# Local q and k in runs of six tokens, put in order on GpSimd, with a one-step scale for the values

## The chip, the cores and the metric

The kernel runs on one core of a Trainium2 chip. The metric is device time in microseconds, the median of three runs of the whole program: 700.77 us before the change (699.4 to 700.79). Five engines work beside each other, each with its own queue in program order: TensorE (PE; its weight loads are listed apart as PEld), VectorE (DVE), ScalarE (ACT), GpSimd (POOL), and SyncE (SP), which issues all DMAs of this kernel.

## What is computed

Attention over 4 batches, 8 heads, 576 tokens and 64 dimensions, with two kinds of mask, feeds two dense blocks. The first four heads are local (a token sees the 32 tokens up to itself); the other four are strided (a token sees the earlier tokens of its residue modulo 32).

```python
scores = scale * np.matmul(q, k.transpose(0, 1, 3, 2))
mask_local = (rel >= 0) & (rel < 32)
mask_strided = (rel >= 0) & (pos[None, :] % 32 == pos[:, None] % 32)
attn = softmax(where(mask, scores, -1e9)); x = attn @ v          # 2304 x 512
h = x @ w_in; sm = softmax(h); solu = h * sm                     # 2304 x 1024
ln = (solu - mu) / np.sqrt(var + 1e-06) * g_ln; y = ln @ w_out   # 2304 x 512
out = (y @ w_a * (y @ w_b)) @ w_out2                             # 512 -> 1536 -> 512
```

## The kernel before

**Tiling.** Attention works on pairs of heads. A `Group` is one batch and one pair, two of each four groups being local and two strided. For each group `load_qk` and `load_v` bring q, k and v into SBUF; `group_T` turns q and k on the PE (`rawq`, `rawk` to `qkT`, six transposes each, then a copy by ACT out of PSUM, L618 for local and L615 for strided groups); `att_tile` makes the scores (L696, L701), the softmax (DVE L719, L728, L732, L736, L738; ACT L731), the product with 1/sum on POOL (`e<-e,r`, L768 in batch 0, L777 later), the transposed probabilities `PT`, and the product with v on the PE into `xbank`. ACT copies this into `xT` (L825). In batch 0 the probabilities are transposed on the PE (L764) and copied by ACT (L774). In batches 1 to 3 they and v are each split into two f16 parts, `PT` comes by a transposing DMA, and v must first be scaled by a power of two.

**The scale of v.** `pair_scale`, once for every two groups of batches 1 to 3 (six times), reduces |v| over each partition into `am` (L630) and calls `pow2_scale`: a transpose on the PE (L500), a maximum on DVE (L501), a second transpose (L505), a second maximum (L506), three DVE instructions on one number (L511 to L513), a matmul that spreads the result over the partitions (L515), and a DVE product (L516). The PE writes these into `scp`, the upper part of the bank `xbank`, beside the attention products in its lower part `x`. The scale of the output weights (`scale_wout`) goes through the same steps once.

**After attention.** `moe1` takes 128 tokens from `xT`: ACT writes `xh` (L845) and DVE `xl` (L849), and 24 matmuls make `h` (L856). DVE, ACT and POOL form softmax, solu and normalisation (DVE L861, L871, L876); a transposing DMA brings `lnT`, and 96 matmuls for every 256 tokens make `y` (L910). The last stage multiplies by a Strassen-like scheme (L1326, L1472). Weights arrive as raw words: each piece of 512 KB goes through a ring of three buffers (`raw64`), is issued at L454, and converted by ACT (L455) and DVE (L461, L465); the pieces of `w_in` are then split by ACT (L474) and POOL (L475).

**Order.** `P.schedule` emits all operations in the order of the table `ISSUE`, which was written ahead of time. Each engine runs its share of that order without overtaking, so an instruction that waits holds all that stands behind it on its engine.

**Local loads before.** `load_qk` brings a local group by one DMA for each head and tensor: 96 partitions, six tokens in each, the tokens of one partition 96 apart, so a run in memory is one token of 256 B. Local transposes then read `rawq` and `rawk` at once.

Of the kernel before, what the change touches and what calls it, by code (L numbers as in the profile page):

```python
# [8 lines left out]
F32 = mybir.dt.float32  # L9
# [21 lines left out]
QT = 96  # L31
# [21 lines left out]
PARAM = dict(back=12, first=40, early=(0,), seed=4, noise=0.1, direct=((0, 0), (0, 1)), stay=0.0, pf1=(),  # L53
             pf2=(), ph1=(), pv=(), pp=(8,), ps1=(), ps2=(), ps3=False, ps4=False, passes=200, ysub=False, wsum=False, osum=False, plo2=(), so=(0, 1, 2), bM=8, bN=4, e=3,
             PT=3, raw=2, rawl=2, raws=2, qkT=2, V=2, wk=2, xt=1, ln=2, lnT=2, ys=2, raw64=3, f64f=4, att=100.0,
# [1572 lines left out]
```

## Time and profile before

| what | us |
|---|---|
| median of three runs | 700.77 |
| the profiled execution | 695.03 |
| its span, first to last instruction | 693.3 |
| PE busy in the span | 664.4 (96%) |
| DVE, ACT, POOL busy | 571.5, 447.2, 144.7 |

The profiled execution is 5.74 us shorter than the median of the timed runs. The page gives busy time for each engine; the windows give the same for a stretch, with the clock that the PE was granted (1.00 stands for 2.4 GHz, 0.50 for 1.2 GHz) and the DMA engines' busy share and rate; the timeline gives single instructions and, in brackets, the idle time ahead of one with what ended it.

### The profile page before, as it was taken

How to read it: one execution, taken by the hardware profiler on the slowest of the kernel's cores; microseconds unless marked ns; L12 is line 12 of the kernel's file. 1: busy time of each engine (PE TensorE's matmuls, PEld its weight loads, DVE VectorE, ACT ScalarE, POOL GpSimd, SP SyncE). 2: the span in 40 equal slices, each digit the busy share in tenths (PEclk: the TensorE clock that was granted, in tenths of full speed). 3: DMA queues.
4: the chain of work that ended last, by engine and by line, in shares of the span. 5: the costliest groups of instructions: out<-in, count | busy, mean ns of one | idle time of the engine just before them, and what ended most of it. 6: DMA issues, size and time to landing. Idle time of an engine off the chain costs nothing.

```text
span 693.3 us, 15572 instructions
## 1 busy us (share of the span) xinstructions
PE 664.4 (96%) x5991; PEld 498.8 (72%) x5991; DVE 571.5 (82%) x1238; ACT 447.2 (65%) x898; POOL 144.7 (21%) x268
## 2 busy tenths in 40 slices
PE   5987899999999999999999999999999999999997
PEld 4766677878787888886576676766767676775676
DVE  5789899789678644999999999799977989786576
ACT  3679868777767644986978787676543746434421
POOL 5544546536537432410000000000000000000000
PEclk9999899999999999999999999999999999999999
DMA  9999979999998434677254043653522304641023
GB/s 209 258 243 244 188 138 194 264 186 268 222 248 199 102 81 102 188 249 240 103 184 152 0 141 104 198 201 97 175 100 94 120 32 166 237 138 46 1 92 122
DMA packets 152650, 109.68 MB, mean 158 GB/s; under 512 B 101376, under 2 KB 131072, under 8 KB 152576
## 3 DMA queue, kind: packets, MB, share of 16 engines
q1 hardware_dynamic: 152576, 108.69, 60.4%
q8 instruction: 47, 0.77, 0.5%
q14 instruction: 27, 0.22, 0.1%
HBM read 65.41 MB, written 27.53 MB: 134 GB/s over the span
## 4 chain that ended last, share of the span: by engine, by line
PE 61%; DVE 8%; ACT 5%; issue 1%; POOL 0%; ACTq 0%; POOLq 0%
PE N L1326 17%; PE M L1326 13%; PE N L1472 9%; PE y L910 7%; PE M L1472 7%; PE h L856 6%; ACT y L1267 1%; DVE p L1423 1%; ACT w L1128 1%; DVE w L1132 1%; DVE y L1269 1%; DVE A L1415 1%; DVE A L1393 1%; DVE V L647 0%; ACT Z L1238 0%
## 5 line engine op out<-in xcount | busy, mean ns | idle before, releaser
L1326 PEld LDWEIGHTS <-w 128*128 128x128 f16 x1512 | 147.9, 98 | 91.7 <-issue 2.0
L1326 PE MATMUL N<-y,w 128*128 128x384 f16 x864 | 156.2, 326 | 0.7 <-ACT N L1333 0.7
L1472 PEld LDWEIGHTS <-p 128*128 128x128 f16 x1071 | 104.7, 98 | 20.4 <-issue 1.1
L1326 PE MATMUL M<-y,w 128*128 128x384 f16 x648 | 118.5, 326 | 0.8 <-ACT N L1333 0.8
L910 PE MATMUL y<-lnT,wout 128*128 128x256 f16 x864 | 101.4, 273 | 1.5 <-DMA lnT<-ln 0.8
L910 PEld LDWEIGHTS <-wout 128*128 128x128 f16 x864 | 82.0, 98 | 15.2 <-issue 4.1
L1418 ACT CAST p<-A 128x384 f16<-128x384 f32 x119 | 59.2, 512 | 40.1 <-DVE A L1393 22.6
L856 PE MATMUL h<-win,xh 128*128 128x512 f32 x288 | 79.8, 417 | 2.7 <-DVE wk L871 2.6
L1472 PE MATMUL N<-wo,p 128*128 128x256 f16 x612 | 77.7, 273 | 1.0 <-DVE yst L1488 1.0
L856 PEld LDWEIGHTS h<-win,xh 128*128 128x128 f32 x288 | 54.4, 198 | 14.4 <-DVE wk L871 3.3
L1423 DVE TENSOR_TENSOR p<-A,p 128x384 f16<-128x384 f32 x119 | 62.3, 552 | 2.7 <-ACT p L1418 2.7
L1472 PE MATMUL M<-wo,p 128*128 128x256 f16 x459 | 60.2, 273 | 0.0
L455 ACT ACTIVATE f64f<-raw 128x512 f32<-128x512 f32 x52 | 34.6, 674 | 11.2 <-DMA raw<-in_moe_w_in_dram 7.3
L856 PE MATMUL h<-win,xl 128*128 128x512 f32 x144 | 39.2, 394 | 0.0
L1415 DVE TENSOR_TENSOR A<-A 128x384 f32<-128x384 f32 x72 | 39.0, 553 | 0.2
L1488 DVE SCALAR_TENSOR_TENSOR ob<-M,osc,ob 128x256 f32<-128x256 f32 x63 | 27.8, 477 | 12.6 <-PE M L1472 11.1
L777 POOL TENSOR_TENSOR e<-e,r 128x324 f32<-128x324 f32 (+2 forms) x30 | 26.2, 881 | 50.0 <-DVE r L738 28.2
L861 DVE TENSOR_REDUCE st<-h 128x1 f32<-128x1024 f32 x18 | 22.0, 1220 | 17.2 <-PE h L856 17.1
L856 PEld LDWEIGHTS h<-win,xl 128*128 128x128 f32 x144 | 26.7, 188 | 5.9
L465 DVE SCALAR_TENSOR_TENSOR f64f<-f64f,raw 128x512 int32<-128x512 int32 x36 | 28.8, 804 | 2.3 <-ACT f64f L455 1.8
L1348 ACT COPY V<-M 128x384 f32<-128x384 f32 x36 | 17.0, 473 | 20.0 <-PE M L1326 19.9
L871 DVE SCALAR_TENSOR_TENSOR wk<-h,st,wk 128x1024 f32<-128x1024 f32 x18 | 23.0, 1279 | 7.8 <-POOL st L869 7.7
(191 smaller groups left out, 1207.0 us busy)
## 6 DMA issues: line engine op xcount, KB each, us to landing
raw<-in_moe_w_out_dram SPq DMA_DIRECT2D x20, 512.0 KB
o_scr<-ob SPq DMA_DIRECT2D x36, 256.0 KB
ob<-o_scr SPq DMA_DIRECT2D x30, 256.0 KB
raw<-in_moe_w_a_dram SPq DMA_DIRECT2D x12, 512.0 KB
raw<-in_moe_w_b_dram SPq DMA_DIRECT2D x12, 512.0 KB
y_scr<-y SPq DMA_DIRECT2D x14, 384.0 KB
y<-y_scr SPq DMA_DIRECT2D x14, 384.0 KB
y_scr<-ys SPq DMA_DIRECT2D x18, 256.0 KB
```

The lines of the kernel that those rows point to most:

```text
L455: act(0.67, lambda: nc.scalar.activation(f(), raw()[:, :, 1].bitcast(F32), AF.Prelu, scale=2.0 ** -112, alpha=-2.0 ** 32), (raw,), (f,))
L465: dve(0.77, lambda: nc.vector.scalar_tensor_tensor(g().bitcast(I32), f().bitcast(I32), 3, raw()[:, :, 0], op0=ALU.logical_shift_left, op1= ...
L777: pool(0.1 + 1.2 * pl, lambda: nc.gpsimd.tensor_tensor(ev(), ev(), r()[:, :ng].unsqueeze(2).to_broadcast([128, ng, nk]), op=ALU.mult), (r, ...
L856: nc.tensor.matmul(h()[:, 512 * n:512 * n + 512], xs[xa]()[:, kk], win[wa][:, kk, 512 * n:512 * n + 512], start=(pi == 0 and kk == 0), sto ...
L871: dve(1.3, lambda: nc.vector.scalar_tensor_tensor(e(), h(), st()[:, 7:8], e(), op0=ALU.mult, op1=ALU.mult, accum_out=st()[:, 2:3]), (h, (s ...
L910: nc.tensor.matmul(y()[:, 256 * mi:256 * mi + 256], wout[:, kk, wa, 128 * m:128 * m + 128], lnT()[:, xa, kk], start=(pi == 0 and kk == 0), ...
L1326: nc.tensor.matmul(to()[:, :HB], w()[:, wa, a, kk], y7[b]()[:, xa, kk], start=first and pi == 0 and kk == 0, stop=pi == 2 and kk == 1, ski ...
L1415: dve(TD, lambda: nc.vector.tensor_tensor(to(), x(), y(), op=op), toks, (to,))
L1418: act(0.5, lambda: nc.scalar.copy(pu(0, a), x()), (x,), (pu.tok(0, a),))
L1423: dve(TD, lambda: nc.vector.tensor_tensor(pu(1, a), x(), pu(0, a), op=ALU.subtract), (x, pu.tok(0, a)), (pu.tok(1, a),))
L1472: nc.tensor.matmul(bk(i), pus[u](xa, a)[:, 128 * tt:128 * tt + 128], wo()[:, u, b, wa], start=a == A11 and u == 0 and pi == 0, stop=u == U ...
L1488: dve(0.475, lambda: nc.vector.scalar_tensor_tensor(dst(), bk(i), s(), dst(), op0=ALU.mult, op1=ALU.add), (src, osc), (obt(t, c),))
```

## The change

A local group's q (and k) comes by one DMA: a partition gets six tokens that follow each other, so a run in memory is 1536 B. GpSimd copies the 96 x 768 block into a new buffer `rawx` with the heads side by side, the transposes read `rawx`, and the ACT copy out of PSUM puts the tokens in order. `rawx` has one buffer, used in turn by q and k of every local group: 16 copies in all. `pair_scale` no longer calls `pow2_scale`: two matmuls against a block of ones sum the partitions' maxima, so that each partition has the sum at once, and four DVE instructions make the power of two and its inverse. The PE output of both now stands in the ring `x`, one buffer that it shares with the attention products. `scale_wout` keeps its steps but also uses `x`. Estimates of PE times in the planner's calls are a little higher, and the table `ISSUE` is new from end to end: of its numbers nothing can be read; what it moves is shown below.

```diff
+    ring("at", "rawx", [QT, 2 * NM * D], F32, pm["rawx"])
...
-    ring("psR", "x", None, F32, 1).fixed = lambda n: xbank[:, :352]
-    ring("psR", "scp", None, F32, 1).fixed = lambda n: xbank[:, 352:]
+    ring("psR", "x", None, F32, 1).fixed = lambda n: xbank
...
-            for h in range(2):
-                dma(lambda t=t, h=h, src=src: nc.sync.dma_start(
-                    out=tokens(t)[:, :, h], in_=src[h].rearrange("(m p) d -> p m d", p=QT)), (), ((t, h),), 190000)
+            src = src.rearrange("h (p m) d -> p h (m d)", p=QT)
+            dma(lambda t=t, src=src: nc.sync.dma_start(out=t().rearrange("p (h n) -> p h n", h=2), in_=src),
+                (), ((t, 0), (t, 1)), 225000)
...
+            if not g.strided:
+                flat, raw = raw, rings["rawx"].new()
+                pool(0.95, lambda flat=flat, raw=raw: nc.gpsimd.tensor_scalar(
+                    raw().rearrange("p (m h d) -> p m h d", m=NM, h=2), flat().rearrange("p (h m d) -> p m h d", h=2, m=NM),
+                    1.0, 1.0, op0=ALU.mult, op1=ALU.mult), ((flat, 0), (flat, 1)), ((raw, 0), (raw, 1)))
...
-                    nc.scalar.activation(dst.rearrange("p (i t) -> p i t", i=2), src, AF.Copy, scale=sc)
+                    nc.scalar.activation(dst.rearrange("p (w i o) -> p w i o", i=2, o=NM // 2),
+                                         src.rearrange("p i (o w) -> p w i o", w=QT), AF.Copy, scale=sc)
...
-        pow2_scale(am, (am,), len(gs), 0, sc, sc)
+        tp, m1 = rings["x"].new(), rings["m1"].new()
+
+        def total():
+            for i in range(len(gs)):
+                nc.tensor.matmul(tp()[:, :1], ones_sq, am()[:, i:i + 1], start=i == 0, stop=i == len(gs) - 1)
+        pe(0.3, total, (am, "small"), (tp,))
+        dve(0.15, lambda: nc.vector.tensor_scalar(m1().bitcast(I32), tp()[:, :1].bitcast(I32), 0x7F800000, None,
+                                                  op0=ALU.bitwise_and), (tp,), (m1,))
+
+        def powers():
+            up, down = sc()[:, 0:1], sc()[:, 1:2]
+            nc.vector.tensor_scalar(down, m1(), 2.0 ** -14, 2.0 ** -60, op0=ALU.mult, op1=ALU.max)
+            nc.vector.reciprocal(up, down)
+            nc.vector.tensor_scalar(down, down, 1.0 / PSCALE, None, op0=ALU.mult)
+        dve(0.4, powers, (m1,), (sc,))
...
 ISSUE = [int(n) for n in """
-10 0 13 11 14 5 2 15 16 1 12 6 18 17 21 8 35 19 9 20 7 4 22 414 37 430 3 771 787 36 39 38 40 43 41 42 181 187 23 66 44
```

The line numbers behind the changed functions shift: by up to 16 from `att_tile` on (L774 is L790 in the changed kernel, L825 is L841, L845 is L861, L856 is L872, L803 is L819), and by one ahead of it (L455 is L454, L474 is L473).

The first place is ACT's queue ahead of the first `xh`, the input of the first `h`. In these rows `raw_407` and the like are raw weight pieces in the order of loading, `e` probabilities, `PT` transposed probabilities. The kernel before:

```order
L474 CAST win_108<-f64f 128x512
L774 COPY PT<-y 96x512
L455 ACTIVATE f64f<-raw_543 128x512
L731 ACTIVATE e_116<-e_116 128x192
L825 ACTIVATE xT<-xbank 128x256
L845 CAST xh<-xT 128x512
L474 CAST win_108<-f64f 128x512
L455 ACTIVATE f64f<-raw_619 128x512
```

Here `raw_543` is the eighth and last piece of `w_in` and `raw_619` the first of the output weights; the second one's conversion comes five rows further on. The changed kernel:

```order
L473 CAST win_108<-f64f 128x512
L454 ACTIVATE f64f<-raw_578 128x512
L790 COPY PT<-y 96x512
L747 ACTIVATE e_115<-e_115 128x384
L841 ACTIVATE xT<-xbank 128x256
L454 ACTIVATE f64f<-raw_628 128x512
L861 CAST xh<-xT 128x512
```

`raw_578` and `raw_628` are the first and second piece of the output weights. The conversions of both now stand ahead of the first `xh`; before, that of the eighth `w_in` piece was the last ahead of it.

The second place is the PE's queue at the first scale of v (batch 1). `am` holds the partitions' maxima, `ident` the identity, `m` the reduced maxima. Before, at the end of the third `h` and behind it:

```order
L856 MATMUL h<-win_108,xl 128x512 x4
L608 MATMUL s<-ident,rawq 128x96 x6
L500 MATMUL xbank<-ident,am 2x128
L798 MATMUL xbank<-PT,rawl 64x64 x2
L608 MATMUL s<-ident,rawk 128x96 x6
L505 MATMUL xbank<-ident,m_1184 1x2
```

The spreading matmul follows after two groups of scores and four matmuls of the fourth `h`:

```order
L701 MATMUL s<-qkT 64x96 x8
L856 MATMUL h<-win_108,xh 128x512 x4
L515 MATMUL xbank<-row,ones 128x2
L856 MATMUL h<-win_109,xh 128x512 x4
L856 MATMUL h<-win_108,xl 128x512 x4
L856 MATMUL h<-win_108,xh 128x512 x4
```

In the changed kernel, from inside the third `h` on:

```order
L872 MATMUL h<-win_108,xh 128x512 x4
L609 MATMUL s<-ident,rawx 128x96 x6
L639 MATMUL xbank<-am,ones 128x1 x2
L872 MATMUL h<-win_109,xh 128x512 x4
L872 MATMUL h<-win_108,xl 128x512 x4
L609 MATMUL s<-ident,rawx 128x96 x6
L639 MATMUL xbank<-am,ones 128x1 x2
```

Three PE steps with DVE work between them have become one. The step of the first pair of batch 1 now stands inside the third `h`, that of the second pair right behind it; two groups of scores later the first product with scaled v follows (L819), ahead of the fourth `h`.

## Rows read from the trace of the kernel before

**Rows 1.** The page: the span, and busy time and share of three engines.
```profile
span 693.3 us, 15572 instructions
...
PE 664.4 (96%) x5991; PEld 498.8 (72%) x5991; DVE 571.5 (82%) x1238; ACT 447.2 (65%) x898; POOL 144.7 (21%) x268
```

**Rows 2.** Windows: stretch in us, length, busy by engine, PE clock, DMA share, GB/s.
```profile
4.20:43.80 39.60, 32.16 (x407) 26.25 (x407) 27.76 (x70) 22.97 (x46) 20.21 (x35) 1.00 1.07 246
...
65.40:67.40 2.00, 0.07 (x1) 0.00 (x0) 1.95 (x5) 2.00 (x6) 1.79 (x4) 0.99 1.08 297
67.40:71.00 3.60, 3.56 (x9) 2.84 (x10) 3.57 (x9) 3.60 (x8) 2.10 (x5) 0.53 0.91 154
71.00:83.00 12.00, 9.56 (x106) 7.04 (x104) 10.03 (x27) 10.09 (x21) 8.32 (x15) 0.92 1.18 212
83.00:87.00 4.00, 4.00 (x15) 2.96 (x16) 3.93 (x12) 3.51 (x6) 0.50 (x1) 0.82 1.14 144
...
104.00:260.00 156.00, 152.49 (x1886) 124.74 (x1884) 119.91 (x242) 110.95 (x209) 79.15 (x149) 1.00 0.93 196
...
400.00:550.00 150.00, 150.00 (x1081) 105.58 (x1080) 131.57 (x311) 98.10 (x222) 0.00 (x0) 1.00 0.43 141
```

**Rows 3.** Windows of the same columns over three slices of the early stage.
```profile
52.00:69.30 17.30, 13.68 (x181) 10.61 (x179) 16.12 (x32) 17.06 (x37) 7.92 (x18) 0.94 1.09 245
69.30:86.70 17.40, 14.96 (x122) 11.10 (x121) 15.36 (x40) 15.01 (x29) 9.64 (x16) 0.86 1.11 188
...
104.00:121.30 17.30, 15.97 (x265) 13.13 (x263) 17.23 (x39) 14.72 (x30) 11.57 (x17) 1.00 1.14 195
```

**Rows 4.** Timeline of ACT: start, duration, instruction, idle before it and releaser.
```profile
34.29 0.68 ACT L455 ACTIVATE f64f<-raw 128x512 f32<-128x512 f32 x1 [2.24 <-DMA raw<-in_moe_w_in_dram]
...
42.60 0.62 ACT L845 CAST xh<-xT 128x512 fp32r<-128x512 f32 x1
...
43.91 0.68 ACT L455 ACTIVATE f64f<-raw 128x512 f32<-128x512 f32 x1
...
47.73 0.66 ACT L455 ACTIVATE f64f<-raw 128x512 f32<-128x512 f32 x1
```

**Rows 5.** Timeline of SP: issue of the first two output-weight pieces.
```profile
37.78 0.35 SPq L454 DMA_DIRECT2D raw<-in_moe_w_out_dram  x1
...
40.69 0.35 SPq L454 DMA_DIRECT2D raw<-in_moe_w_out_dram  x1
```

**Rows 6.** Timeline of PE: parts of the first h; first product with scaled v.
```profile
43.80 3.52 PE L856 MATMUL h<-win,xh 128*128 128x512 f32 x8
...
48.06 1.98 PE L856 MATMUL h<-win,xh 128*128 128x512 f32 x8
...
88.37 0.20 PE L803 MATMUL xbank<-PT,V 54*64 54x54 f16 x2
```

**Rows 7.** Waits of PE from 43 to 260 us: total, times, longest.
```profile
PE xbank L505 <- DVE m L501: 1.1, 2, 0.7
PE xbank L500 <- DVE sc L516: 1.0, 2, 0.5
PE xbank L803 <- DVE sc L516: 1.0, 2, 0.6
...
PE xbank L515 <- DVE row L513: 0.5, 1, 0.5
```

**Rows 8.** Groups by line and form, 0 to 270 us: count, busy us, mean ns, idle.
```profile
L465 DVE SCALAR_TENSOR_TENSOR f64f<-f64f,raw 128x512 int32<-128x512 int32 x20 | 18.0, 898 | 2.2 <-ACT f64f L455 1.8
...
L465 DVE SCALAR_TENSOR_TENSOR wout<-f64f,raw 128x512 int32<-128x512 int32 x8 | 5.5, 686 | 0.6 <-ACT f64f L455 0.5
```

**Rows 9.** The same view of POOL, whole span, products with 1/sum.
```profile
L768 POOL TENSOR_TENSOR e<-e,r 128x384 f32<-128x384 f32 x4 | 3.9, 984 | 3.8 <-DVE r L738 2.2 <-PE y L764 1.7
```

**Rows 10.** Groups of ACT by form, whole span: copies of q and k out of PSUM.
```profile
L615 ACT ACTIVATE qkT<-s 128x576 f32<-128x576 f32 x16 | 10.2, 647 | 6.9 <-PE s L608 6.9
L618 ACT ACTIVATE qkT<-s 128x576 f32<-128x576 f32 x16 | 10.1, 644 | 0.1
```

More of the change, by code (lines that the diff above doesn't have):

```diff
@@ L51 @@
 PASSES = ((0, 0), (0, 1), (1, 0))
-PARAM = dict(back=12, first=40, early=(0,), seed=4, noise=0.1, direct=((0, 0), (0, 1)), stay=0.0, pf1=(),
+PARAM = dict(scp="x", back=12, first=40, early=(0,), seed=4, noise=0.1, direct=((0, 0), (0, 1)), stay=0.0, pf1=(),
              pf2=(), ph1=(), pv=(), pp=(8,), ps1=(), ps2=(), ps3=False, ps4=False, passes=200, ysub=False, wsum=False, osum=False, plo2=(), so=(0, 1, 2), bM=8, bN=4, e=3,
-             PT=3, raw=2, rawl=2, raws=2, qkT=2, V=2, wk=2, xt=1, ln=2, lnT=2, ys=2, raw64=3, f64f=4, att=100.0,
+             PT=3, rawx=1, raw=2, rawl=2, raws=2, qkT=2, V=2, wk=2, xt=1, ln=2, lnT=2, ys=2, raw64=3, f64f=4, att=100.0,
              win=24.5, wout=128.6, moff=-69.7, moe=96.6, conv2=257.2, dconv=15.0, p2=385.0, pre=6.5, fine=(),
@@ L493, in load_wout, with pow2_scale @@
             ("g", ("wof", c)), (f, ("wam", c)))
-    def pow2_scale(am, toks, n, unit, dst, dtok, top=14, least=60, ps="scp", sm=""):
-        tp = bank(ps) if ps == "M" else rings[ps].new()
+    def pow2_scale(am, toks, n, unit, dst, dtok, top=14, least=60, ps=None, sm=""):
+        tp = bank(ps) if ps == "M" else rings[ps or pm["scp"]].new()
         m1, row = rings[sm + "m1"].new(), rings[sm + "row"].new()
-        pe(0.12, lambda: nc.tensor.transpose(tp()[:n, :128], am(), ident), (*toks, "ident"), (tp,))
+        pe(0.2, lambda: nc.tensor.transpose(tp()[:n, :128], am(), ident), (*toks, "ident"), (tp,))
         dve(0.27, lambda: nc.vector.tensor_reduce(m1()[:n], tp()[:n, :128], axis=AX.X, op=ALU.max), (tp,), (m1,))
@@ L514, in pow2_scale @@
         dve(0.47, chain, (), (m2, row))
-        pe(0.1, lambda: nc.tensor.matmul(tp()[:, 144:146], ones, row()[:1], start=True, stop=True), (row, "small"), (tp,))
+        pe(0.25, lambda: nc.tensor.matmul(tp()[:, 144:146], ones, row()[:1], start=True, stop=True), (row, "small"), (tp,))
         dve(0.16, lambda: nc.vector.tensor_tensor(dst(), tp()[:, 144:146], units[:, unit], op=ALU.mult), (tp, "small"), (dtok,))
@@ L544, in batch_tiles @@
         return seq + [(g, j) for j in range(len(LT)) for g in loc]
-    def tokens(t):
-        return t().rearrange("p (m h d) -> p m h d", m=NM, h=2)
     def load_qk(g):
@@ L608, in transposes @@
                     nc.tensor.transpose(to, raw()[:, 128 * m:128 * m + 128], ident[:QT, :QT])
-            pe(NM * 0.09, transposes, ((raw, 0), (raw, 1), "ident"), (tp,), 855)
+            pe(NM * 0.09 + 0.05, transposes, ((raw, 0), (raw, 1), "ident"), (tp,), 855)
             def evac(c=c, tp=tp):
@@ L704, in att_tile @@
         if not (g.strided and j):
-            pe(2 * npb * nk * 0.42e-3 + sum(4 * kk / 2.4e3 + 0.01 for kk in groups) + 0.03, scores,
+            pe(2 * npb * nk * 0.42e-3 + sum(4 * kk / 2.4e3 + 0.01 for kk in groups) + 0.1, scores,
                ((g.T, 0), (g.T, 1), "identb", "masks" if g.strided else "maskl"), [(sp, f) for f in range(2)],
@@ L769, in att_tile @@
                                                            op=ALU.mult), (r, *ee), (e,))
-            pe(nblk * 0.14, transposes, (tok, "ident"), (pt,), nblk * rows * 2)
+            pe(nblk * 0.15 + 0.05, transposes, (tok, "ident"), (pt,), nblk * rows * 2)
             def evac():
@@ L806, in att_tile @@
         if direct:
-            pe(sum(4 * c[5] / 2.4e3 + (0.06 if g.strided else 0.015) for c in cells if not c[0]), pv, (PT, *g.vtoks), (x,),
+            pe(sum(4 * c[5] / 2.4e3 + (0.06 if g.strided else 0.015) for c in cells if not c[0]) + 0.07, pv, (PT, *g.vtoks), (x,),
                1.3 * sum(2 * c[5] * nk / 128 for c in cells), 1)
         else:
-            pe(sum(3 * c[5] / 2.4e3 + (0.035 if g.strided else 0.015) for c in cells if not c[0]), pv, (PT, *g.V), (x,),
+            pe(sum(3 * c[5] / 2.4e3 + (0.035 if g.strided else 0.015) for c in cells if not c[0]) + 0.07, pv, (PT, *g.V), (x,),
                1.27 * sum(1.5 * c[5] * nk / 128 for c in cells), 1)
@@ L858, in mm @@
                                          start=(pi == 0 and kk == 0), stop=(pi == 2 and kk == 3))
-                s1_ops.append(pe(4 * 0.230, mm, [xs[xa]] + [((("win", kk, n), wa)) for kk in range(4)], (h,), 2048))
+                s1_ops.append(pe(4 * 0.237, mm, [xs[xa]] + [((("win", kk, n), wa)) for kk in range(4)], (h,), 2048))
         st, e, ln = rings["st"].new(), rings["wk"].new(), rings["ln"].new()
@@ L928, in scale_ab @@
         x, y = wab[:, u, 0, m:m + 1], wab[:, u, 1, m:m + 1]
-        pe(0.12, lambda: nc.tensor.matmul(tp()[:, :2], ones_sq, fro[:, u, m], start=True, stop=True),
+        pe(0.22, lambda: nc.tensor.matmul(tp()[:, :2], ones_sq, fro[:, u, m], start=True, stop=True),
            [("fro", u, m, i) for i in range(2)] + ["small"], (tp,), 8)
```

262 rows, old and new, of the table ISSUE are left out of this document.

## Prediction

> **What bounds the kernel now.** I read the page first: the PE is busy for 664.4 of 693.3 us [rows 1], so all that any change of order can win is the 29 us in which it idles and the stretches in which it runs slowly. The windows then say where these lie. From 104 to 260 us it idles 3.5 us, from 400 to 550 us not at all [rows 2]. In the last tenth of the program the changed table leaves the engines' order almost as it was. So the change must win or lose ahead of some 100 us. There the PE idles 7.4 us between 4.2 and 43.8, 1.9 us at 65.4 to 67.4, and 2.4 us from 71 to 83 [rows 2]. The clock column adds something: right after the idle 2 us the granted clock is 0.53 for 3.6 us, and it is below 1.00 again from 71 to 87 [rows 2]. Lost PE time there is 0.47 x 3.6 + 0.08 x 12 + 0.18 x 4 = 3.4 us. Two more things are to be seen: the DMA engines are full (share 1.07) up to 43.8 us [rows 2], and from 52 to 121 us DVE is 88% to 100% busy, ACT up to 99% [rows 3]. The early stage is thus bound by DMA first, then by DVE and ACT, and only later by the PE.
>
> All sums below are against the profiled execution, 695.03 us; the timed median is 5.74 us higher, and I carry that difference over to the end unchanged.
>
> **The loads.** Local q and k of a batch are 2 groups x 2 tensors x 2 heads x 147,456 B = 1.18 MB. At the rate of the full early stretch, 246 / 1.07 = 230 GB/s for a full share, they take 5.1 us; at the slowest early row, 154 / 0.91 = 169, 7.0 us; at the rate of the late stage, whose transfers run long, 141 / 0.43 = 328, 3.6 us [rows 2]. The change therefore frees 1.5 to 3.4 us of DMA time in batch 0; I take 2.5, since the old runs of 256 B were the shortest in that mix. In batches 1 to 3 the same saving exists, but no PE wait there names q or k, so I count nothing for it; if that cover were gone it would be 2.5 us a batch at most. SP saves 16 issues, none of them on the path.
>
> That time does not reach the first `h` whole, because the order moved too. Before, `xh` began at 42.60, the second output-weight piece was issued at 40.69 and converted at 47.73 without a wait on its DMA [rows 4, 5]; so it landed between those two times. Its neighbour was issued 2.9 us earlier and had landed by 43.91, which puts this one at 46.8 at the latest by the same spacing. I take 45. In the changed order its conversion stands ahead of `xh`. With 2.5 us freed it lands at 42.5, its conversion takes 0.67, and `xh` begins at 43.2: the first `h` is **0.6 us later**, not earlier. Ends: 2.5 us earlier, if all that `xh` waits for comes sooner by the time freed, and 46.23 + 0.67 - 42.60 = 4.3 us later, if it lands at 47.73 less 1.5.
>
> In exchange two pieces are converted by the time that the first `h` appears: 2 x 0.69 us of L465 on DVE and 2 x 0.67 on ACT [rows 4, 8]. DVE idled 11.8 us from 4.2 to 43.8 [rows 2] and hardly after, so this work leaves the full stretch. Worth **-1.5 us** (0 to -2.8, if the shorter DVE step of each piece, L461, is taken as long as L465).
>
> **The scale of v.** The PE waited 1.1 + 1.0 + 1.0 + 0.5 = 3.6 us for steps of this chain [rows 7]. Two of its three PE steps go for all six pairs; the one that is left can still wait, for `am`, and now also for the copy of the last attention product out of `x`, behind which all PE work is queued. I take half, **-1.8 us** (0 to -3.6). DVE's count falls by two instructions a pair, which I price at nothing. The first product with scaled v, at 88.37 before [rows 6], moves ahead of the fourth `h`. It stands two score groups behind the new matmul, so if the two parts of V are late the PE stands there; that is the upper end 0 of this term.
>
> **The copies on POOL.** No row shows a one-input copy of 768 columns. The nearest is the product of 384 columns with two inputs, 0.98 us [rows 9]: by columns that makes 1.97, by elements read 0.98. I take 1.0, so 16 us in all, on an engine that is busy 144.7 of 693 [rows 1]. Up to 43.8 it had 19.4 us idle [rows 2], and the four copies of batch 0 fit there. What they cost others: while POOL works, DVE's L465 takes 0.898 against 0.686 in the stretch where it wrote `wout` and POOL was quieter [rows 8], 20 x 0.212 = 4.2 us for 144.7 us of POOL. At that rate 16 copies cost 0.5 us; if each held up one such instruction, 16 x 0.212 = 3.4. I take **+0.4**, nearer to the mean than to the worst. With one `rawx` buffer the copy of k waits for the transposes of q; the PE has scores and products to do between them, and so I add nothing, though up to 0.5 us for each of the eight local groups could show.
>
> The ACT copy out of PSUM reads with a stride now. Strided groups already write theirs with one, and take 0.647 us against 0.644 for local ones [rows 10]; I price the stride at nothing. If the read cost the same time again, it would be 4 x 0.64 = 2.6 us of ACT a batch; the upper end takes that in.
>
> **Sum.** +0.6 - 1.5 - 1.8 + 0.4 = -2.3 us: 692.7 for a profiled execution, 698.5 for the median.
>
> **Rivals.** (a) *The start waits for weights, slower.* `xh` now stands behind a transfer that it did not need. If the piece lands at its latest, the first `h` is 4.3 us later instead of 0.6, and the scale gives back only what its lower half says, 0.9: +4.3 - 1.5 - 0.9 + 0.4 = +2.3, median 703.1. For it: DMA is full, and ACT already waited 2.24 us on a piece at 34.29 [rows 4]. Against it: the ring lets the piece be issued sooner if DVE converts earlier ones sooner, which the new order does. It decides from about 3 us of delay on.
>
> (b) *Copies lock DVE out, slower.* The eight copies of batches 1 and 2 fall into the stretch where DVE is 88% to 100% busy. If each stopped DVE for its whole 0.98 us, that is 7.8 us; +0.6 - 1.5 - 1.8 + 7.8 = +5.1, median 705.9. The rows bear it out only in part: 0.212 us is what one L465 loses on average beside POOL [rows 8]. It decides from 2.7 us in all on. The Trainium skill, page "SBUF — State Buffer", section "SBUF: two separate sides", holds it for the rule: the two engines share a port pair, which one of them keeps for a whole instruction while the other blocks fully, if DVE runs in a two-port mode or reads two SBUF inputs. The trace agrees in sign, by the 0.898 against 0.686 us, not in size.
>
> (c) *No change.* From 52 to 121 us DVE and ACT are the bound [rows 3] and their counts hardly change. An earlier V and freed DMA time then turn into other waits: 0, median 700.8.
>
> (d) *More.* If v's scale comes early enough, the PE waits of 65 to 83 us are filled, the clock stays at 2.4 GHz, and the 3.4 us of slow PE come on top: -5.7, median 695.1. The level is worth that much: eight matmuls of `h` took 3.52 us in the cold start and 1.98 a little later [rows 6].
>
> **How the numbers follow.** The forecast has 0.36, (a) 0.17, (b) 0.08, (c) 0.24, (d) 0.15. A measurement of this kernel tells about 0.2%, 1.4 us, from no change: so faster means below 699.4, slower above 702.2. Faster is the forecast and (d), 0.51; the same is (c), 0.24; slower is (a) and (b), 0.25. The forecast's own range is 697 to 700. The whole one reaches down to (d) with the 2.5 us of the loads' lower end, 692.5, and up to (a) with half of the 2.6 us of a slower ACT copy, 704.5; (b) is left out.
>
> **What would show it.** Right: the first `h` at 43 to 45 us; no PE wait on the scale chain over 0.5 us; the first product with V some 10 us ahead of 88; PE idle ahead of 104 us down by about 2 us; POOL copies near 1.0 us; the time from 260 us on unchanged in length. Wrong: the first `h` after 46 (a); L465 and its like well over 0.9 us in 52 to 121 us (b); a PE wait on V of some us in the third `h`; or a clock below 1.00 in other places than before. The new table moves hundreds of instructions that I have not priced one by one; if PE idle after 104 us grows beyond the 3.5 us it had, that is where the forecast failed.

## The result and the profile after

The changed kernel takes 708.99 us (median of 4, 708.73 to 711.15) against 700.09 us (697.65 to 700.79) for the kernel before on the same chip: a ratio of 1.014, with an interval of 1.0115 to 1.0164. The forecast was 698.5 us; the time lies outside its range, on the other side.

First the page of the changed kernel, answering [rows 1]:

```profile
span 707.0 us, 15549 instructions
...
PE 667.3 (94%) x5991; PEld 499.7 (71%) x5991; DVE 573.7 (81%) x1226; ACT 449.2 (64%) x898; POOL 162.5 (23%) x284
```

The PE does the same 5991 matmuls, is busy 2.9 us longer and idles 39.7 us of the span instead of 28.9. Some 1.1 us of the 2.9 are a slow clock (0.09 x 50.38 = 4.5 us from 43.8 to 104 us, by the rows below, against the 3.4 of the prediction). Most of the loss is idle time. Windows say where it lies; columns as in [rows 2], first the changed kernel, then a second profiled execution of the kernel before (span 694.8 us, run as `before_again`):

```profile
4.20:43.80 39.60, 28.81 (x363) 22.65 (x364) 23.39 (x55) 20.34 (x40) 21.41 (x36) 1.00 1.04 238
43.80:104.00 60.20, 50.38 (x602) 39.84 (x601) 55.65 (x121) 49.64 (x99) 29.38 (x46) 0.91 0.85 206
104.00:260.00 156.00, 150.91 (x1866) 124.20 (x1865) 121.63 (x236) 108.55 (x203) 88.89 (x156) 1.00 0.87 190
260.00:400.00 140.00, 135.06 (x976) 98.89 (x975) 119.99 (x246) 104.49 (x190) 19.38 (x39) 1.00 0.50 159
```
```profile
4.20:43.80 39.60, 31.01 (x404) 25.42 (x405) 26.07 (x68) 22.87 (x45) 20.55 (x34) 0.89 1.10 242
43.80:104.00 60.20, 51.86 (x601) 40.26 (x600) 52.06 (x115) 46.58 (x91) 25.83 (x46) 0.90 0.99 195
104.00:260.00 156.00, 153.17 (x1892) 125.30 (x1891) 121.75 (x244) 112.45 (x211) 80.98 (x150) 1.00 0.92 198
260.00:400.00 140.00, 137.72 (x989) 101.40 (x987) 127.54 (x261) 106.46 (x196) 14.23 (x30) 1.00 0.47 151
```

By PE busy time (the first number behind the length) the changed kernel loses 2.2, 1.5, 2.3 and 2.7 us in the four stretches: no single place, and 4.9 of these 8.6 us lie behind 104 us, where the forecast saw nothing to win or lose. Against the first profile of before it loses 3.4, 2.7, 1.6 and 2.7, that is 10.3 us, 4.3 of them behind 104 us.

The first `h` starts at 50.81 us instead of 43.80 [rows 6]. Around it, SP of the changed kernel and SP of the kernel before at the same loads, then ACT and PE of the changed kernel, answering [rows 4 to 6] (start, duration, instruction, idle time and releaser):

```profile
17.60 6.47 SPq L566 DMA_DIRECT2D rawl<-in_v_dram  x4
24.18 2.17 SPq L453 DMA_DIRECT2D raw<-in_moe_w_in_dram  x1
```
```profile
20.27 0.35 SPq L454 DMA_DIRECT2D raw<-in_moe_w_in_dram  x1
20.66 3.88 SPq L570 DMA_DIRECT2D rawl<-in_v_dram  x4
```
```profile
39.33 0.69 ACT L454 ACTIVATE f64f<-raw 128x512 f32<-128x512 f32 x1 [2.07 <-DMA raw<-in_moe_w_in_dram]
...
48.45 0.67 ACT L454 ACTIVATE f64f<-raw 128x512 f32<-128x512 f32 x1 [0.20 <-DMA raw<-in_moe_w_out_dram]
49.02 0.61 ACT L861 CAST xh<-xT 128x512 fp32r<-128x512 f32 x1
```
```profile
50.81 2.67 PE L872 MATMUL h<-win,xh 128*128 128x512 f32 x8
...
89.64 0.26 PE L819 MATMUL xbank<-PT,V 54*64 54x54 f16 x2 [0.64 <-DVE m L641]
```

SP needs 6.47 us for four loads of v, and the fifth `w_in` piece, behind them, goes out only at 24.18. In the kernel before, the fifth piece stood ahead of these loads and went out at 20.27. Pieces then come late one after the other, ACT waits for them, and `xh`, behind the second output-weight piece, starts at 49.02 instead of 42.60.

Answering [rows 7 to 10], the waits of the PE from 43 to 260 us that name the scale, and the groups of the conversions (first 270 us), copies and ACT's evictions (whole span):

```profile
PE xbank L514 <- DVE row L512: 1.3, 1, 1.3
...
PE xbank L819 <- DVE m L641: 0.6, 1, 0.6
```
```profile
L464 DVE SCALAR_TENSOR_TENSOR f64f<-f64f,raw 128x512 int32<-128x512 int32 x20 | 18.5, 924 | 3.6 <-ACT f64f L454 2.8 <-DMA rawl<-in_v_dram 0.3
```
```profile
L619 ACT ACTIVATE qkT<-s 128x576 f32<-128x576 f32 x16 | 10.3, 641 | 1.3 <-PE s L609 1.2
L597 POOL TENSOR_SCALAR rawx<-rawq 96x768 f32<-96x768 f32 x8 | 7.9, 994 | 5.3 <-DMA rawq<-in_q_dram 5.3
L597 POOL TENSOR_SCALAR rawx<-rawk 96x768 f32<-96x768 f32 x8 | 7.1, 884 | 2.2 <-issue 1.4 <-POOL win L474 0.5 <-PE s L609 0.2
```

The scale chain's waits fell from 3.6 to 0.6 us for v (L514 is now the scale of the output weights alone, which kept the old chain; its wait of 1.3 us is new), copies take 0.88 to 0.99 us, L464 rose from 898 to 924 ns, and the strided read of the evictions costs nothing (641 against 644 ns). Each of these terms came out near the forecast. What was lost lies in none of them.

### The profile page after: what moved, and what is told of

Read it like the earlier page. It is cut to its first block, busy times and chain, and to the rows that moved or that the text cites. A ratio compares the mean times of both kernels' runs of the same rounds, so it can differ in the third digit from the quotient of the medians.

```text
span 707.0 us, 15549 instructions
## 1 busy us (share of the span) xinstructions
PE 667.3 (94%) x5991; PEld 499.7 (71%) x5991; DVE 573.7 (81%) x1226; ACT 449.2 (64%) x898; POOL 162.5 (23%) x284
## 4 chain that ended last, share of the span: by engine, by line
PE 50%; DVE 21%; ACT 3%; DMA 2%; issue 2%; POOL 0%; SPq 0%; DVEq 0%; ACTq 0%; POOLq 0%
PE N L1342 14%; PE M L1342 9%; PE N L1488 8%; PE M L1488 6%; PE h L872 5%; PE y L926 5%; DVE p L1439 2%; DVE y L1285 2%; DVE w L1148 2%; DVE S L1134 1%; DVE A L1409 1%; DVE wo L1227 1%; DVE A L1431 1%; DMA raw<-in_moe_w_out_dram 1%; DMA PT<-P 1%
## 5 line engine op out<-in xcount | busy, mean ns | idle before, releaser
L872 PE MATMUL h<-win,xh 128*128 128x512 f32 x288 | 79.3, 414 | 3.3 <-DVE wk L887 3.1
L872 PEld LDWEIGHTS h<-win,xh 128*128 128x128 f32 x288 | 54.1, 197 | 15.5 <-PE y L926 1.5
L454 ACT ACTIVATE f64f<-raw 128x512 f32<-128x512 f32 x52 | 34.9, 676 | 18.6 <-DMA raw<-in_moe_w_in_dram 10.7
L872 PE MATMUL h<-win,xl 128*128 128x512 f32 x144 | 39.5, 396 | 0.0
L793 POOL TENSOR_TENSOR e<-e,r 128x324 f32<-128x324 f32 (+2 forms) x30 | 29.2, 980 | 31.5 <-DVE r L754 23.4
L464 DVE SCALAR_TENSOR_TENSOR f64f<-f64f,raw 128x512 int32<-128x512 int32 x36 | 29.3, 820 | 3.6 <-ACT f64f L454 2.8
L892 DVE SCALAR_TENSOR_TENSOR ln<-wk,st,ln 128x1024 f16<-128x1024 f32 x18 | 24.7, 1370 | 8.5 <-ACT ln L891 8.3
L872 PEld LDWEIGHTS h<-win,xl 128*128 128x128 f32 x144 | 26.6, 188 | 5.6
L1504 DVE SCALAR_TENSOR_TENSOR ob<-N,osc,ob 128x256 f32<-128x256 f32 x45 | 20.5, 481 | 12.2 <-PE N L1488 11.0
```

The lines of the kernel that those rows point to most:

```text
L454: act(0.67, lambda: nc.scalar.activation(f(), raw()[:, :, 1].bitcast(F32), AF.Prelu, scale=2.0 ** -112, alpha=-2.0 ** 32), (raw,), (f,))
L464: dve(0.77, lambda: nc.vector.scalar_tensor_tensor(g().bitcast(I32), f().bitcast(I32), 3, raw()[:, :, 0], op0=ALU.logical_shift_left, op1= ...
L793: pool(0.1 + 1.2 * pl, lambda: nc.gpsimd.tensor_tensor(ev(), ev(), r()[:, :ng].unsqueeze(2).to_broadcast([128, ng, nk]), op=ALU.mult), (r, ...
L872: nc.tensor.matmul(h()[:, 512 * n:512 * n + 512], xs[xa]()[:, kk], win[wa][:, kk, 512 * n:512 * n + 512], start=(pi == 0 and kk == 0), sto ...
L892: dve(1.3, lambda: nc.vector.scalar_tensor_tensor(ln()[:, 1], e(), st()[:, 3:4], ln()[:, 0], op0=ALU.add, op1=ALU.subtract), (e, (st, 3), ...
L1504: dve(0.475, lambda: nc.vector.scalar_tensor_tensor(dst(), bk(i), s(), dst(), op0=ALU.mult, op1=ALU.add), (src, osc), (obt(t, c),))
```

## The experiments

Theory 1 at first: the edits are worth what the forecast said, and the new table of issue numbers loses the time. The rival: the edits themselves cost it, above all the copies. "In the order of before" means that the table was rebuilt, so that every instruction that both kernels have stands where it stood before.

**The edits without the new order.** The code is the changed one, but v's scale keeps its own columns of the bank, since the sharing would force an order of its own:

```diff
-    ring("psR", "x", None, F32, 1).fixed = lambda n: xbank
+    ring("psR", "x", None, F32, 1).fixed = lambda n: xbank[:, :352]
+    ring("psR", "scp", None, F32, 1).fixed = lambda n: xbank[:, 352:]
```

> The changed code (loads in runs of six tokens, copies on GpSimd, scale from a matmul sum) in the order of the kernel before: each new instruction stands where the one it replaces stood, and each copy eight places ahead of its transposes; v's scale keeps the columns of its own in the PSUM bank. Theory 1 (the new order costs the time, the edits do not): 696 to 700 us, first product of h at 42 to 45 us as before (43.8) and not at 50.8. Theory 2 (the edits themselves cost it: copies beside DVE, loads, the strided read): 705 to 710 us, first h near 50.

`loads_old_order` puts the old scale back into this code, `scale_old_order` the old loads:

```diff
-        tp, m1 = rings[pm["scp"]].new(), rings["m1"].new()
...
+        pow2_scale(am, (am,), len(gs), 0, sc, sc)
```
```diff
-            src = src.rearrange("h (p m) d -> p h (m d)", p=QT)
...
+            for h in range(2):
```

> Only the loads in runs with their copies and the strided read; the scale of v and the order are those of before. Theory 1: 698.5 to 702 us (some 2 us of DMA time freed, some 0.4 us lost on DVE). Theory 2, if it is the copies: 704 us or more, with DVE's conversion steps beside GpSimd well over 0.9 us in 52 to 121 us. Theory 2, if it is the scale: no change from before.

> Only the new scale of v; loads and order are those of before. Theory 1: 697 to 700 us, between no change and the 3.6 us that the PE waited for this chain. Theory 2, if it is the scale (its matmuls in 32-bit floating point, or V coming late): 703 us or more.

Measured: both edits 1.0074 (1.0042 to 1.0105), loads alone 1.0105 (1.0051 to 1.0158), scale alone 0.9980 (0.9953 to 1.0006). So neither theory holds as written: with both edits the time is that of theory 2, the first `h`, at 43.62, that of theory 1. Loads with copies lose in the old order too; the scale loses nothing, and whether it gains is open here, since its interval includes no change. Half of the 1.4% would then be left for the new order, but only if the edits lose as much there as in the old one; the runs below show that they do not. In `edits_old_order` the PE waits for copies, and a long pause is followed by a slow clock. Its waits from 43 to 215 us (total, times, longest), then its windows around one of the waits for a copy, 1.93 us that end at 155.31:

```profile
PE s L610 <- POOL rawx L598: 4.2, 3, 1.9
PE s L718 <- ACT qkT L617: 3.3, 2, 3.1
```
```profile
152.00:156.00 4.00, 2.07 (x48) 1.84 (x48) 3.41 (x9) 2.02 (x4) 3.81 (x6) 0.92 0.37 94
156.00:160.00 4.00, 4.00 (x68) 2.92 (x68) 0.19 (x2) 2.60 (x6) 2.43 (x6) 0.50 0.25 50
160.00:164.00 4.00, 4.00 (x81) 3.34 (x73) 2.82 (x5) 3.19 (x8) 0.00 (x0) 0.72 0.93 134
```

The PE idles 1.9 us, and then the granted clock is 0.50 (the lower level) and on average 0.72 over 8 us in which it is always busy: 0.50 x 4.00 + 0.28 x 4.00 = 3.1 us more. In the kernel before, the clock is 1.00 from 136 to 164 us. So this pause took some 5 us of PE time, two and a half times its length.

**The new order with the old loads.** The copies and the `rawx` ring go, the two loads of 256 B runs a tensor come back:

```diff
-                flat, raw = raw, rings["rawx"].new()
-                pool(0.95, ...)
```

> The new order and the new scale with the loads of before (runs of 256 B, two transfers a tensor, no copies on GpSimd; seven loads stand later, since their buffer is now held until the transposes). Theory 1: 706 to 712 us, first h at 49 us or later. Theory 2, if it is loads and copies: 699 to 702 us, first h at 44 us.

Measured 1.0216 (1.0155 to 1.0276), above even what theory 1 expected: the new order is worse still with the old loads. It was made for a buffer that is free after the copy; seven loads had to stand later here, so this is not a clean price of the loads.

**Copies off the PE's path.** The copy of k goes into the buffer which the copy of q has emptied, and the copies stand earlier:

```diff
-                flat, raw = raw, rings["rawx"].new()
+                flat, raw = raw, g.raw[0] if c else rings["rawx"].new()
```

> The changed code in the order of before, as in edits_old_order, but the copy of k goes into the buffer that the copy of q has just emptied, and in batches 1 to 3 the copies stand 22 places ahead of their transposes instead of 8. So no copy waits for the PE any more, and the PE should not wait for a copy. Theory 1 (what edits_old_order lost is the PE's wait for rawx, 4.9 us, and the slow clock after each such pause): 697 to 700 us, no PE wait for a copy over 0.5 us, and no clock of 0.50 near 82 and 151 us. Theory 2 (the copies cost by slowing DVE): 704 us or more, as in edits_old_order (705.7).

`runs_no_copy` keeps the loads in runs and drops these lines, so that local tokens stay out of order:

> As copies_apart (loads in runs, new scale, order of before) but without any copy on GpSimd: the transposes read the loaded tile as it lies, so the tokens of the local heads are not put in order, and only the time counts. Theory 1 (what is left of the loss, 1.0045 against the 0.998 of the scale alone, are the copies): 0.995 to 0.999 of before. Theory 2 (it is the loads: transfers that land at other moments behind full DMA queues): 1.003 to 1.006, as copies_apart.

`copies_alone` adds sixteen copies to the kernel before, which nothing reads:

```diff
+                rx = rings["rawx"].new()
+                pool(0.95, lambda flat=raw, rx=rx: nc.gpsimd.tensor_scalar(...
```

> The kernel before with sixteen copies added on GpSimd, placed as in copies_apart, into a tile that nothing reads; loads, scale and order are those of before. Theory 1 (the copies slow what runs beside them, DVE above all): 1.004 to 1.008 of before. Theory 2 (the copies cost only where someone waits for them): 0.998 to 1.002.

Measured: 1.0045 (1.0021 to 1.0070), 0.9973 (0.9941 to 1.0004) and 1.0024 (0.9998 to 1.0049); the first and the third lie between their theories. So in the order of before the loads in runs show neither a cost nor a gain beside the scale's 0.998. The copies' work costs some 0.24%, 1.7 us, which the interval does not quite separate from nothing. What is left, by differences of the medians, is put down to the PE's dependence on the copies: another 3 us in `copies_apart`, where one wait of 3.0 us for a copy remained against the expectation, and 5 us in `edits_old_order`.

**Copies cut short in the new order.** Each copy moves 4 of every 64 columns; the tile is set to zero once at the start.

```diff
-raw().rearrange("p (m h d) -> p m h d", m=NM, h=2)
+raw().rearrange("p (m h d) -> p m h d", m=NM, h=2)[:, :, :, :4]
```

> The changed kernel in the new order with each copy cut to 48 of 768 columns (4 of each 64), so that all waits and places stay and the copies' work goes; the local q and k are then mostly zeros, and only the time counts. Theory 1 (copies about 0.7%, order about 0.7%): 1.006 to 1.009 of before. Theory 2 (in the new order the copies find room and cost nothing): 1.012 to 1.015. Theory 3 (the copies are all of the loss): 0.998 to 1.002.

Measured 1.0137 (1.0107 to 1.0166), the changed kernel's own time. With this the copies' work is out as a cause of the 1.4%: the new order hides it, and loses 1.4% without it. The hand-over through GpSimd stays in this run; `all_old_short` below has it too, and takes the time of before.

**The start.** Two runs exchange parts of the table ahead of the first `h`. `weights_behind`, on ACT (the DVE steps of the same two pieces and one load move with them):

```diff
 L473 CAST win_108<-f64f 128x512
-L454 ACTIVATE f64f<-raw_578 128x512
 L790 COPY PT<-y 96x512
 L747 ACTIVATE e_115<-e_115 128x384
 L841 ACTIVATE xT<-xbank 128x256
-L454 ACTIVATE f64f<-raw_628 128x512
 L861 CAST xh<-xT 128x512
 L747 ACTIVATE e_116<-e_116 128x192
+L454 ACTIVATE f64f<-raw_578 128x512
+L454 ACTIVATE f64f<-raw_628 128x512
```

> The changed kernel with one thing moved: the five conversion steps (two on ACT, three on DVE) of the first two output-weight pieces, that stand ahead of the first xh and xl, go behind them, and the one load that waits for their buffer moves with them. Theory 1 (these pieces hold the first h): first h at 45 to 47 us instead of 50.8, total 704 to 706 us. Theory 2 (the input-weight pieces come late already, since SP stands at other loads ahead of them): first h at 49 to 51 us, total 707 to 709 us.

`old_head` takes the whole start of the table from before, with no other edit:

> The changed kernel with every engine's order up to the first product of h taken from before (copies included as in edits_old_order), and the new order behind that. Theory 1 (the new order loses its time in the start, and what is lost later follows from that): first h at 43 to 45 us, total 699 to 703 us. Theory 2 (the new order loses as much after the start, at 185 to 365 us): first h at 43 to 45 us, total 705 to 709 us.

Measured 1.0205 (1.0175 to 1.0235) and 1.0133 (1.0098 to 1.0169). Theory 1 falls in both (the first run, at 713.37 us, lies beyond its theory 2 as well). Behind `xh` the two conversions cost 0.65% more, and the first `h` came no sooner (52.1 us), so these pieces do not hold it. With the old start the first `h` is at 43.95, 6.9 us earlier than in the changed kernel, for the same total. The PE's timeline of `old_head` shows where it went:

```profile
43.95 2.54 PE L872 MATMUL h<-win,xh 128*128 128x512 f32 x8
...
58.68 0.66 PE L780 MATMUL y<-ident,e 128*96 128x128 f32 x2 [6.99 <-ACT PT L790]
```
```profile
4.20:104.00 99.80, 78.70 (x966) 63.21 (x967) 79.22 (x175) 70.63 (x138) 51.05 (x81) 0.88 0.91 219
```

The 7 us are waited at 51.7 to 58.7 instead, for attention's `PT` from ACT, which stands there behind conversions of output weights. The changed kernel does that attention work ahead of its first `h`. So the idle time was moved, not won: from 4.2 to 104 us the PE is busy 78.7 us in `old_head` and 79.2 in the changed kernel, against 82.9 in `before_again`. The wait stands where one order gives way to the other, so this run does not tell what the new start costs by itself.

**The rest of the order, cut in two at some 215 us.** The table is spliced, and v's scale keeps its own columns: all rows up to `h` number 11 by one table, all others by the other.

> The changed kernel (v's scale with columns of its own) in the new order up to h number 11, that is up to about 215 us, and in the order of before behind that. Theory 1 (the new order loses both ahead of 104 us, some 6 us, and at 300 to 400 us, 2.3 us of PE idle time): 1.009 to 1.012 of before, with PE idle time from 300 to 400 us at 1.5 to 2 us again. Theory 2 (nearly all of it goes early): 1.013 to 1.015.

> The reverse: the order of before with the copies as in edits_old_order up to h number 11, the new order behind that. Theory 1: edits_old_order (1.0074) plus the 2.3 us of 300 to 400 us, 1.009 to 1.012. Theory 2 (the new order's second part costs nothing): 1.006 to 1.009. A time above 1.013 would say that most of the new order's loss lies behind 215 us.

Measured 1.0173 (1.0134 to 1.0212) and 1.0157 (1.0115 to 1.0199): both lie outside their theories, both halves lose, and the sum is more than the whole. The second expectation took a time above 1.013 to put most of the loss behind 215 us; the first run says as much for the front, so neither can be read that way. In `new_then_old` the PE idles 6.7 us from 180 to 300 us, behind the seam at some 215 us, where the changed kernel idles 1.5. A seam, the place where one order gives way to the other, can cost by itself; such runs do not price a part.

**The tail.** At some 265 us both orders have done the same work but for one instruction, so the seam is clean; the table alone is spliced:

> The changed kernel with the order of before from about 265 us on (both orders have done the same work there, but for one instruction). Theory 1 (the 2.2 us of extra PE idle time at 300 to 400 us come from the new order there): 1.010 to 1.012 of before, with PE idle time from 300 to 400 us at 1.5 to 2 us. Theory 2 (they come from something earlier, and only show there): 1.013 to 1.015.

Measured 1.0080 (1.0050 to 1.0110): the old order behind 265 us gives 0.6%, 4.2 us, back, more than theory 1 expected. This is the first cause that is shown. DVE's queue there, the changed kernel and then `old_tail`:

```
L1353 TENSOR_TENSOR A<-N_4871,V 128x384
L1213 TENSOR_TENSOR S<-yst 128x256
L1213 TENSOR_TENSOR S<-yst,S 128x256
L1213 TENSOR_TENSOR S<-yst 128x256
L1213 TENSOR_TENSOR S<-yst,S 128x256
L1353 TENSOR_TENSOR C<-N_5080,V 128x384
```
```
L1353 TENSOR_TENSOR A<-N_4850,V 128x384
L1227 SCALAR_TENSOR_TENSOR wo<-yst,small,wo 128x2x256
L1227 SCALAR_TENSOR_TENSOR wo<-yst,small,wo 128x256
L1227 SCALAR_TENSOR_TENSOR wo<-S,small,wo 128x4x256
```

In the trace of the changed kernel, DVE's waits from 300 to 360 us, the PE's work that they name, and the windows of the two kernels, the changed one first:

```profile
DVE C L1353 <- PE N L1342: 4.0, 1, 4.0
DVE S L1213 <- DMA yst<-w_scr: 3.1, 2, 2.7
DVE A L1353 <- PE N L1342: 2.7, 2, 2.3
```
```profile
315.62 5.40 PE L926 MATMUL y<-lnT,wout 128*128 128x256 f16 x48
320.86 2.11 PE L1342 MATMUL N<-y,w 128*128 128x384 f16 x12
322.81 5.40 PE L926 MATMUL y<-lnT,wout 128*128 128x256 f16 x48
```
```profile
320.00:330.00 10.00, 10.00 (x82) 7.82 (x80) 2.64 (x6) 2.32 (x4) 0.00 (x0) 1.00 0.81 270
...
300.00:400.00 100.00, 95.88 (x691) 66.73 (x690) 89.06 (x184) 77.48 (x147) 5.49 (x9) 1.00 0.48 166
```
```profile
320.00:330.00 10.00, 10.00 (x77) 7.33 (x75) 9.57 (x23) 6.99 (x16) 0.00 (x0) 1.00 0.84 281
...
300.00:400.00 100.00, 98.20 (x713) 68.99 (x711) 98.07 (x204) 81.76 (x156) 4.75 (x9) 1.00 0.48 161
```

From 300 to 400 us the old order keeps PE and DVE both nearly full: 98.20 and 98.07 us in `old_tail`, 98.14 and 98.24 in the kernel before. The other runs say the same, whatever they do ahead of it: the six kernels with the new order in this stretch have PE at 95.9 and DVE at 89.0 to 89.1, the fourteen with the old one 98.0 to 98.5 and 97.8 to 98.3. In the changed kernel `A` and `C` wait at the head of DVE's queue for products `N` that stand on the PE behind 48 matmuls of `y`, and `S` waits for a transfer; what DVE could do meanwhile is queued behind. It loses 9 us while the PE is busy, so nothing shows there. The PE pays some 25 us later (its waits from 330 to 372 us, then those of `old_tail`):

```profile
PE M L1342 <- DVE y L1285: 1.3, 2, 0.8
PE M L1342 <- ACT N L1349: 0.6, 1, 0.6
PE N L1342 <- ACT N L1349: 0.5, 1, 0.5
PE N L1342 <- DVE A L1353: 0.5, 1, 0.5
PE M L1342 <- ACT y L1283: 0.5, 1, 0.5
```
```profile
PE M L1342 <- ACT N L1349: 0.8, 1, 0.8
```

From 260 to 400 us the PE is busy 138.2 us in `old_tail` and 135.1 in the changed kernel. These 3.1 us are nearly the whole difference of the two spans, 703.7 and 707.0. That the order behind 265 us causes it is shown by the run; that `A`, `C` and `S` at the head of DVE's queue are the reason is read from the traces, and no run moved them alone.

**Ahead of 265 us.** Three runs of one code (copies cut short) differ in the order alone: all old, new up to 110 us, new from 110 to 265 us.

> The changed code with copies cut to 48 of 768 columns (local q and k mostly zeros, only the time counts; v's scale with PSUM columns of its own), wholly in the order of before. Theory 1 (the copies' own work, and the PE's wait for it, are what edits_old_order lost): 0.996 to 1.000 of before, as runs_no_copy. Theory 2 (the further hand-over through GpSimd costs, however short the copy): 1.003 to 1.006.

> The same code, in the new order up to h number 4 (some 110 us), then in the order of before. Theory 1 (the start of the new order loses, by the PE idle time of 0 to 104 us, 24.8 against 21.0 us): 0.4 to 0.8% above all_old_short. Theory 2 (that idle time is given back later): within 0.2% of all_old_short.

> The same code, in the order of before up to h number 4 (some 110 us), in the new order up to some 265 us, then in the order of before. Theory 1 (the middle of the new order loses little): within 0.4% of all_old_short. Theory 2 (it loses what the changed kernel's PE idles more from 104 to 180 us, 2.5 to 3.1 us): 0.4 to 0.8% above all_old_short.

Measured 1.0011 (0.9974 to 1.0047), 1.0047 (1.0019 to 1.0074) and 1.0157 (1.0121 to 1.0193). The first, between its theories, says that this code in the old order takes the time of before. In the new order it took 1.0137 (`short_copies`, the same but for the bank of v's scale), so 1.26% are the order. Sharing the bank goes with it and had no run of its own; but `new_then_old` and `old_then_new` do not share it and, seams and copies included, lose no less than the changed kernel. The second run puts the start at 0.36%, with intervals that overlap. The third lies outside both theories and is more than the whole changed kernel with its old tail (1.008), so the seam at its start may well cost by itself. Its waits from 104 to 140 us name transfers that come late for the new middle:

```profile
PE xbank L823 <- DMA PT<-P: 2.3, 2, 1.6
PE y L930 <- DMA lnT<-ln: 2.0, 1, 2.0
```

So of the 1.4%, 0.6% are shown to come from the order behind 265 us, with a mechanism seen in the traces; the other 0.8% are left, by elimination, to the order ahead of it, spread over the start and the middle. Which instructions there are to blame stays open.

**A kernel that beats both.** The scale alone, once more:

> scale_old_order once more, over more rounds: only the new scale of v in the kernel before. From the first time (0.998, 0.9953 to 1.0006): 0.996 to 1.000 of before. If the scale were what costs in the changed kernel, it would be above 1.003.

Measured 697.37 against 699.85 us, 0.9966 (0.9941 to 0.9991). With the first time, 0.9980, the new scale of v is worth 1.4 to 2.4 us in the order of before (only the second interval excludes no change), and this kernel is the best here. And the plain kernel before:

> The kernel before, unchanged, to see what another profiled execution of it looks like. Theory 1 (the first profile, 695.0 us, was of a quick execution; a usual one takes 699 to 700 us and has the pauses near 53 us too, followed by a slow clock): span 696 to 700 us, PE idle 32 us or more instead of 28.9, and h number 4 at 113 to 115 us instead of 110.4. Theory 2 (the first profile is typical in its stages): idle near 29 us, h number 4 within 1 us of 110.4.

Ratio 0.9982 (0.9948 to 1.0015), span 694.8 us, 30.4 us of PE idle time: nearer to theory 2, though `h` number 4 starts 2.2 us later, between the two. The first profile was hardly luckier than the second; both executions were quicker than their medians (695.03 against 700.09, 696.60 against 698.62).

## Why the prediction was wrong

**What failed first is the bounding step.** "In the last tenth of the program the changed table leaves the engines' order almost as it was. So the change must win or lose ahead of some 100 us." The first sentence is true, the second does not follow: between 104 us and the last tenth the table moved hundreds of instructions. The argument was that the PE hardly idles there [rows 2], so nothing can be *won*. But a stretch without idle time is one in which a new order can only *lose*, and 4.9 of the 8.6 us of lost PE time lie there (4.3 of 10.3 against the first profile). Ahead of 104 us the sum of -2.3 us met a loss of 3.7 to 6.0. The last paragraph of the prediction named this as the place where it would fail, and gave it no price and no chance. PE idle time from 104 to 260 us grew from 3.5 to 5.1 us, as that paragraph feared, and the first `h` came after 46, its sign of (a).

**The loads, +0.6 us (ends -2.5 and +4.3).** Wrong twice. In size: the first `h` came 7.0 us later, not 0.6. The bound of 4.3 looked at one piece in ACT's queue; SP's queue, where v's loads moved ahead of a `w_in` piece, was not walked. In meaning: the place of the first `h` was taken for the place of the end. `old_head` brought it back without a gain. A milestone tells time only if the work ahead of it is the same; the PE's idle time tells more. From 4.2 us to its first `h` the changed kernel idles 13.0 us, the two profiles of before 7.4 and 8.6. So 4.4 to 5.6 of the 7.0 us are idle time and the rest is attention done ahead; what the start costs in the end is not told apart (0.36%, 2.5 us, by `new_to_110`). The 2.5 us of freed DMA time bought nothing that shows either: `runs_no_copy` takes as long as the scale alone.

**Conversions done ahead, -1.5 us (0 to -2.8).** The right sign; with `weights_behind` their place is worth 0.65%, 4.6 us, in this order. Part of that may be the load that moved with them, which was not told apart.

**The scale, -1.8 us.** Right: 0.9980 and 0.9966, that is -1.4 and -2.4 us, and the chain's waits for v fell to 0.6 us (beside a new one of 1.3 us for the output weights). But the first product with scaled v did not come 10 us sooner; it is at 89.64 instead of 88.37.

**The copies, +0.4 us.** Size of one: right, 0.83 to 1.0 us. Their price is some 1.7 us in the old order, if any, and nothing that shows in the new one. The 0.5 us for each local group, named and left out, was real where the order did not care: in `edits_old_order` the PE waited 4.2 us, and the clock fell behind it. The strided eviction at nothing: right.

**The rivals.** (a) had the place (a start that waits for weights) and an end on the right side, but not the cause that it names: with the output-weight pieces behind `xh` the first `h` came no sooner. A late start is part of the loss, and its price is not told apart. (b) is refuted as a cause by `short_copies`, and (c) and (d) by the time itself. The two rows that (d) gives for the worth of the clock, 3.52 and 1.98 us, do not show it: the granted clock reads 1.00 at both. Missing was a rival of its own for the table: that an order made new as a whole loses in a stretch where PE and DVE are both full.

**Its measure and sums.** It took 0.2% to be told from no change; single times of the kernel before lay between 693.27 and 705.28 us over the experiments, and even ten runs leave some 0.3%. Two slips in the whole range do not matter here: with +0.6 replaced by -2.5 its lower end is 692.0, and its upper end adds up to 704.4.

## What to carry to other kernels

When a change brings a new order with it, price the order as a change of its own, over every stretch where rows moved, and most of all where the critical engine has no idle time: there it can only lose. Walk there the queue of the second-busiest engine, here DVE at 98%, and look for instructions at its head that wait for work which has moved back on another engine. The cheapest first experiment is the new code in the old order; here it leads to the one edit worth keeping. It wants its reverse beside it, the new order with the new work cut short, since work that is new has no place in the old order and can cost there what it does not cost in the new.

## What the runs showed of the hardware that was not expected

DVE can stand beside POOL for much longer than the mean of its rows told. In the changed kernel a 128x6 step of 0.17 us and a conversion of 0.69 us stretch to 0.66 and 2.29 (POOL first, then DVE):

```profile
11.85 0.83 POOL L597 TENSOR_SCALAR rawx<-rawq 96x768 f32<-96x768 f32 x1 [2.76 <-DMA rawq<-in_q_dram]
...
22.81 1.00 POOL L597 TENSOR_SCALAR rawx<-rawq 96x768 f32<-96x768 f32 x1
23.79 1.27 POOL L474 TENSOR_TENSOR win<-f64f,win 128x512 fp32r<-128x512 f32 x1
...
80.47 0.83 POOL L597 TENSOR_SCALAR rawx<-rawq 96x768 f32<-96x768 f32 x1
```
```profile
12.04 0.66 DVE L752 SCALAR_TENSOR_TENSOR sm<-sm,over 128x6 f32<-128x6 f32 x1
...
23.31 2.29 DVE L464 SCALAR_TENSOR_TENSOR f64f<-f64f,raw 128x512 int32<-128x512 int32 x1 [0.17 <-ACT f64f L454]
...
80.86 0.47 DVE L748 TENSOR_REDUCE sm<-e 128x6 f32<-128x324 f32 x1
```

L752 ends at 12.70, when the copy ends (12.68); L464 ends 0.54 us after POOL's second instruction (25.06). Both read two SBUF tiles. L748, a reduction of one tile, keeps its 0.47 us beside a copy. This agrees with the full lock that the Trainium skill, page "SBUF — State Buffer", section "SBUF: two separate sides", states for DVE instructions with two SBUF inputs beside a GpSimd instruction that reads SBUF. The prediction weighed it against a mean, and so took the trace to disagree in size. Of the 20 conversions in that mean, four had no POOL instruction beside them, four stood beside short steps of POOL on statistics and kept 0.66 to 0.69 us, while the one beside two products of POOL in a row, at 25.90, took 1.81. In the new order the lock still costs nothing that shows (`short_copies`, 1.0137 against 1.0140).

A slow clock showed little in the time here. In `scale_again` it stood near its lower level from 20 to 43.8 us, while weights were being loaded and the PE idled 6.1 of 23.8 us, and the span was 695.1 us. In the kernel before it was 1.00 over that stretch and the span 693.3; in `before_again` 0.82 and 694.8. What it did cost is not told apart from the scale's gain:

```profile
20.00:43.80 23.80, 17.66 (x228) 14.46 (x229) 16.62 (x40) 15.42 (x31) 13.45 (x12) 0.57 1.10 253
```
